# Loading the last 64 rows of a QKV weight into 128 partitions: one transfer or two

## The chip, the cores and the metric

The kernel runs on one core of one Trainium2 chip. The metric is the device time of one execution in microseconds (us). Five engines work side by side: TensorE (PE, matrix products), VectorE (DVE), ScalarE (ACT), GpSimd (POOL) and SyncE (SP). SP computes nothing here; it issues most of the DMA transfers. A core has 16 DMA engines that carry these transfers.

## The reference

One token stream `x` (1 x 2048 x 576, bf16) is normalised, and the same normalised rows feed a local dilated attention and a SwiGLU feed-forward block. The three are added up.

```python
xn = _layernorm(x)                                  # no gain, no bias
# attention: 32 heads of 18; each position looks at 8 positions, 0, 2, ..., 14 back
qkv = (xn @ wqkv)                                   # wqkv: 576 x 1728
logits = einsum("bhsd,bhswd->bhsw", q, kg) * 18 ** -0.5   # masked before position 0
o = einsum("bhsw,bhswd->bhsd", softmax(logits), vg) @ wo
# feed-forward, F = 4608
ffn = (silu(xn @ w_gate) * (xn @ w_up)) @ w_down
return x + o + ffn
```

The contraction length 576 is four blocks of 128 and a rest of 64. The change is in how the rest of `wqkv`, its rows 512 to 575, gets into the on-chip memory.

## The kernel before, in words

The 2048 positions are held as 128 partitions x 16 rows: partition p has positions 16p to 16p+15, and "row r" is the position r of each partition, 128 positions in all. The kernel first computes Q, K and V for all 16 rows (`p_mm`, L310, until about 59.7 us), then runs four rounds of the feed-forward block (`g_pair`, L611, and `d_half`, L640), with the attention of four rows at a time done on DVE beside it (`chain`, L418 to L465). All instructions are issued in the order written (a manual schedule); DVE's attention steps are put between the others by a small planner (`Filler`) that goes by fixed costs.

What matters here is the first 25 us. The transfers, in the order in which they are issued, will be called:

- x0 (on ACT's queue) and x1, x2, x3 (on SP's): the input's rows 0 to 3, one at a time, `load_x`, L145, 128 partitions of 1152 bytes each.
- w1 (on ACT's queue) and w0, w2, w3 (on SP's): the four 128-row blocks of `wqkv`, `load_w`, L149, 128 partitions of 3456 bytes each.
- w4, the last 64 rows of `wqkv`, L152: two transfers, here w4a and w4b, of 64 partitions of 1728 bytes each. The weight's 1728 columns are cut in two halves of 864. The first half goes to partitions 0 to 63 of the tile `wqkvr`, the second to partitions 64 to 127. So PE can use the upper and the lower half of its rows at the same time, each with other output columns.
- c1, c2, c3: the other 12 input rows, L165, 128 partitions of 4608 bytes each.
- The first feed-forward weights, `load_gu(0)`: gate (L182), up (L183) and the two 64-partition rests g8a and g8b (L184, L185); they are first used at 67.1 us.
- Then two zero fills of the K and V rings (L542), and the transposes of normalised rows by DMA (L300): row 0, which is for later, and rows 5, 6, 7, ..., which PE's Q/K/V products need.

SP's order is x1, w0, w2, x2, w3, w4a, w4b, x3, c1, c2, c3, gate, up, g8a, g8b, the zero fills, the transposes. The program gives the DMA transfers eight semaphores in turn; so a transfer also waits, before it is issued, until the one eight places ahead of it has landed.

PE's order at the start: eleven matmuls on constants (`warm_pe`, L174 and L177), the transposes of row 0 (L271), then row 0's products block by block: `p_whole` for w0, w1 and w2, between them the transposes of row 1, four products of row 1 with w0, then four of row 0 with w3 (at 9.37 us) and, as the first use of w4, four half-height products of row 0 (`p_row0_rest`, from 10.20 us). After that `p_row(1, ...)`, `p_row(2)` and so on, 3.3 us each. In `p_row`, w4 is the second block that is used. The products of row 0 are taken out of PSUM by `p_evac(0, ...)` on ACT and DVE as soon as the four half-height products are done.

```python
    def p_row0_rest(t):
        for i in range(2):
            for half in range(2):
                p_mm(t, i + 2 * half, 4, half, 0, False, True)
```

Of the kernel before, what the change touches and what calls it, by code (L numbers as in the profile page):

```python
# [17 lines left out]
P = 128  # L18
H, DH, W, DIL = 32, 18, 8, 2
D = H * DH  # L20
HALF = D // 2
G = 432
# [48 lines left out]
def kernel(  # L71
# [58 lines left out]
    wqkvr = hTf[:, 12 * D:12 * D + 2 * G]  # L130
# [16 lines left out]
    def load_w(eng, kt):  # L147
        if kt < 4:
            eng.dma_start(wqkv[:, kt, :], A_wqkv[kt * P:(kt + 1) * P, :])  # L149
        else:  # L150
            for i in range(2):
                eng.dma_start(wqkvr[64 * i:64 * i + 64, :], A_wqkv[4 * P:D, 2 * G * i:2 * G * (i + 1)])  # L152

    load_x(nc.scalar, 0)
    load_x(nc.sync, 1)
    load_w(nc.scalar, 1)
    load_w(nc.sync, 0)
    make_identity(nc, ident[:])
    load_w(nc.sync, 2)
    load_x(nc.sync, 2)  # L160
    load_w(nc.sync, 3)
# [562 lines left out]
```

## Time and profile before

| | |
|---|---|
| median of 3 runs | 503.4 us (503.15 to 503.45) |
| the profiled execution | 503.37 us, its span 501.6 us |
| PE busy | 497.6 us, 99% of the span |
| DVE, ACT, POOL busy | 329.3 us (66%), 200.9 us (40%), 2.7 us (1%) |
| DMA, mean over the span | 150 GB/s |
| w4a, w4b: 108 KB each, issue to landing | 5.9 and 6.5 us |

The span runs from the first to the last instruction; the time of an execution has about 1.8 us more. Busy times of PE are modelled from pipelined starts, so 99% says that PE has nearly always a matmul under way, not that each runs at its best rate.

### The profile page before, as it was taken

What the parts mean: (1) busy time and instruction counts of PE and PEld (TensorE: products, weight loads), DVE (VectorE), ACT (ScalarE), POOL (GpSimd) and SP (SyncE); (2) the same over time, 40 slices, a digit from 0 to 9 for tenths busy, and PEclk for the clock granted to TensorE, in tenths of its full rate; (3) what the DMA queues carried; (4) which work ended last, traced back from release to release, by engine and by line L of the source; (5) the groups of instructions that cost most, each with busy time, mean ns of one, the idle gap of its engine ahead of it and who ended that gap; (6) DMA issues with size and microseconds to landing.
All of it is one profiled execution on the core that took longest, in us unless ns stands there. A gap on an engine that the chain in (4) does not pass through costs nothing.

```text
span 501.6 us, 13271 instructions
## 1 busy us (share of the span) xinstructions
PE 497.6 (99%) x5795; PEld 283.1 (56%) x5795; DVE 329.3 (66%) x479; ACT 200.9 (40%) x416; POOL 2.7 (1%) x9
## 2 busy tenths in 40 slices
PE   9999999999999999999999999999999999999997
PEld 4555544444677644444777544445777444446775
DVE  5888597898999698999897139995980222221001
ACT  4756657645300255554300445557000454553000
POOL 1000000000000000000000000000000000000000
PEclk9999999999999999999999999999999999999999
DMA  8799989898731045535640154453700335432200
GB/s 311 175 205 238 306 271 293 259 322 260 194 117 61 25 143 189 190 110 177 158 132 29 31 182 153 132 189 110 183 25 14 101 115 177 158 127 39 76 14 25
DMA packets 77186, 75.42 MB, mean 150 GB/s; under 512 B 22708, under 2 KB 72528, under 8 KB 77128
## 3 DMA queue, kind: packets, MB, share of 16 engines
q1 hardware_dynamic: 76840, 73.98, 49.7%
q8 instruction: 45, 0.74, 0.6%
q10 hardware_dynamic: 288, 0.59, 0.3%
q14 instruction: 13, 0.11, 0.1%
HBM read 58.76 MB, written 5.90 MB: 129 GB/s over the span
## 4 chain that ended last, share of the span: by engine, by line
PE 99%; DVE 0%; issue 0%
PE g_ps L611 56%; PE d_ps L640 32%; PE qkv_ps L310 11%; PE warm_ps L174 1%; PE pt L271 0%; DVE ot L654 0%; PE pt L292 0%; PE warm_ps L271 0%; PE warm_ps L177 0%
## 5 line engine op out<-in xcount | busy, mean ns | idle before, releaser
L611 PE MATMUL g_ps<-xnT,gu 64*128 64x512 bf16 x2592 | 280.4, 376 | 0.0
L611 PEld LDWEIGHTS <-gu 64*128 64x128 bf16 x2592 | 126.1, 94 | 152.9
L622 ACT ACTIVATE sg<-g_ps 128x512 bf16<-128x512 f32 x144 | 87.3, 606 | 156.6 <-PE g_ps L611 156.6
L640 PE MATMUL d_ps<-wd,hT 64*128 64x288 bf16 x2304 | 146.3, 283 | 0.0
L640 PEld LDWEIGHTS <-hT 64*128 64x128 bf16 x2304 | 112.0, 94 | 29.8
L624 DVE TENSOR_TENSOR hT<-sg,uc 128x512 bf16<-128x512 bf16 x144 | 60.2, 419 | 93.9 <-ACT uc L623 93.8
L623 ACT CAST uc<-g_ps 128x512 bf16<-128x512 f32 x144 | 85.2, 592 | 0.0
L423 DVE TENSOR_REDUCE PP<-PP 128x64 f32<-128x1152 bf16 x64 | 84.9, 1347 | 0.4
L310 PE MATMUL qkv_ps<-hT,xnT 64*128 64x432 bf16 (+1 forms) x536 | 50.0, 342 | 0.0
L418 DVE TENSOR_TENSOR PP<-QO,Kr 128x2304 bf16<-128x2304 bf16 (+1 forms) x35 | 43.5, 1251 | 7.3 <-DMA Kr<-hT 6.9
L652 DVE TENSOR_TENSOR ot<-d_ps,xr 128x288 bf16<-128x288 f32 x30 | 12.3, 451 | 51.0 <-PE d_ps L640 51.0
L450 DVE TENSOR_TENSOR PP<-Vr,A 128x2304 bf16<-128x2304 bf16 (+1 forms) x35 | 43.3, 1251 | 0.4
L310 PEld LDWEIGHTS <-xnT 64*128 64x128 bf16 (+1 forms) x536 | 26.1, 94 | 22.3 <-ACT xnT L296 0.2
L455 DVE TENSOR_TENSOR PP<-PP 128x2304 bf16<-128x2304 bf16 x24 | 32.5, 1354 | 0.3
L622 ACT ACT_TABLE_LOAD x5 | 6.4, 1283 | 47.2 <-PE g_ps L611 47.2
L640 PE MATMUL d_ps<-wo,xnT 64*128 64x288 bf16 x288 | 22.9, 283 | 0.0
L372 ACT CAST hT<-qkv_ps 128x288 bf16<-128x288 f32 (+2 forms) x58 | 20.9, 423 | 0.0
L443 ACT ACTIVATE PP<-PP 128x1024 f32<-128x1024 f32 x4 | 4.2, 1056 | 31.3 <-DVE PP L439 31.2
L640 PEld LDWEIGHTS <-xnT 64*128 64x128 bf16 x288 | 14.0, 94 | 3.6
L654 ACT CAST ot<-d_ps 128x288 bf16<-128x288 f32 x1 | 0.4, 399 | 38.8 <-PE d_ps L640 38.8
L372 ACT CAST QO<-qkv_ps 128x432 bf16<-128x432 f32 (+1 forms) x30 | 12.2, 406 | 8.3 <-PE qkv_ps L310 8.2
L221 DVE BATCH_NORM_STATS2 stats<-wd 128x6 f32<-128x288 bf16 x32 | 12.8, 440 | 0.0
(56 smaller groups left out, 92.1 us busy)
## 6 DMA issues: line engine op xcount, KB each, us to landing
gu<-in_B_w_gate_dram SPq DMA_DIRECT2D x36, 512.0 KB, 3.8
gu<-in_B_w_up_dram SPq DMA_DIRECT2D x36, 512.0 KB, 5.2
wd<-in_B_w_down_dram SPq DMA_DIRECT2D x9, 576.0 KB, 6.2
kv_d<-hT SPq DMA_DIRECT2D x5, 576.0 KB, 6.1
gu<-in_B_w_gate_dram SPq DMA_DIRECT2D x36, 64.0 KB, 4.9
gu<-in_B_w_up_dram SPq DMA_DIRECT2D x36, 64.0 KB, 4.5
xr<-in_A_x_dram SPq DMA_DIRECT2D x8, 288.0 KB, 3.9
out_dram<-ot SPq DMA_DIRECT2D x16, 144.0 KB, 1.8
```

The source lines that it names most:

```text
L221: nc.vector.bn_stats(sums[r][:, k, :], xc[:, j, k * HALF:(k + 1) * HALF])
L310: return nc.tensor.matmul(t[g][:, 0:G], xT_of(r)[rows, kt, :], w_at(g, kt, rows), start=start, stop=stop)
L372: (nc.vector.tensor_copy if n in dve else nc.scalar.copy)(*parts[n])
L418: nc.vector.tensor_tensor(prod[:, a:b], QO[:, RT * tt + a:RT * tt + b, :], Kr[:, s:s + b - a, :], op=ALU.mult)
L423: nc.vector.tensor_reduce(L[:, w, rs], prod[:, rs].rearrange("p r (h d) -> p r h d", d=DH), axis=AX.X, op=ALU.add)
L450: nc.vector.tensor_tensor(dst[:, a:b], Vr[:, s:s + b - a, :].rearrange("p r (d h) -> p r d h", h=H), A[:, w, a:b].unsqueeze(2).to_broadcas ...
L455: nc.vector.tensor_tensor(dst, acc, pv, op=ALU.add)
L611: mm = nc.tensor.matmul(ring_ps[j][b][:], gu[rows, slot, k, fc], xnT[rows, kt, tok], start=(swap == 0 and kt == 0), stop=(swap == 1 and kt ...
L622: nc.scalar.activation(sg[:], t[0][:], ACT.Silu)
L623: nc.scalar.copy(uc[:], t[1][:])
L624: nc.vector.tensor_tensor(hT[:, ch * FC + j, :], sg[:], uc[:], op=ALU.mult)
L640: mm = nc.tensor.matmul(t[sub][h][:, 0:HALF], a[rows], w[rows, h * HALF:(h + 1) * HALF], start=(swap == 0 and n == 0), stop=(swap == 1 and ...
```

## The change

The two transfers of w4 become one. The source is viewed as two halves of 64 rows of 864 columns, with the half as the outermost index, and the target is the whole tile of 128 partitions.

```diff
@@ -148,8 +148,7 @@
         if kt < 4:
             eng.dma_start(wqkv[:, kt, :], A_wqkv[kt * P:(kt + 1) * P, :])
         else:
-            for i in range(2):
-                eng.dma_start(wqkvr[64 * i:64 * i + 64, :], A_wqkv[4 * P:D, 2 * G * i:2 * G * (i + 1)])
+            eng.dma_start(wqkvr, A_wqkv[4 * P:D, :].rearrange("r (i c) -> i r c", i=2))
```

In the program that is built, the two transfers of before have a source and a target of 64 x 864 elements each. The one that replaces them has a source of 2 x 64 x 864 and a target of 128 x 1 x 864. No other instruction is added, removed or moved on any engine. With one transfer fewer, those that follow take the next semaphore in turn, and PE waits for one semaphore instead of two before the first use of w4.

## The prediction

> **What bounds the kernel now.** I read first the page's busy times and the chain that ended last, for the engine that sets the time.
>
> ```profile
> PE 497.6 (99%) x5795; PEld 283.1 (56%) x5795; DVE 329.3 (66%) x479; ACT 200.9 (40%) x416; POOL 2.7 (1%) x9
> PE 99%; DVE 0%; issue 0%
> ```
>
> The chain is PE from 0.77 us on, without a step that waits for a DMA. So PE can win almost nothing, and whatever makes it wait has no cover: it goes to the end in full. The question is whether w4 still comes in time. I therefore took the timeline of PE and SP at the start, the line of w4's transfers (L152) with its landing times, and the busy times by stretches.
>
> ```profile
> 8.64 0.89 PE L310 MATMUL qkv_ps<-hT,xnT 128*128 128x432 bf16 x4
> 9.37 1.36 PE L310 MATMUL qkv_ps<-hT,PP 128*128 128x432 bf16 x8
> ...
> 3.07 1.34 SPq L152 DMA_DIRECT2D hT<-in_A_wqkv_dram  x2
> ...
> DMA to landing us min/median/max: 5.9/6.2/6.5
> ...
> 6.80:10.20 3.40, 3.40 (x24) 1.81 (x23) 2.71 (x10) 1.23 (x4) 0.74 (x1) 1.00 1.05 327
> 10.20:13.60 3.40, 3.40 (x47) 1.89 (x48) 2.86 (x9) 2.74 (x8) 0.58 (x1) 1.00 1.02 409
> ```
>
> The eight matmuls at 9.37 are row 0's four with w3 and the four half-height ones with w4, which start at 10.20. The two w4 transfers were issued at 3.07 and 3.95, so they land at 9.59 and 9.89 (the trace's semaphore events say the same): 0.3 us before their use. In the stretches PE is busy throughout, and the DMA engines too (shares 1.05 and 1.02). The transfers are bound by their engines, not by their issue: w4 is issued at 3.1 to 4.4, and its first packet starts at 7.56.
>
> **The change part by part.** The sum is made against the profiled execution: 503.37 us, of which 501.6 span; the median of the runs is 503.4, so its differences carry over as they are.
>
> *Over how many engines w4 is spread.* A landing counts 16 on a semaphore, and the trace shows who counts. Transfers whose outermost index runs over 128, 112 or 64 climb by 16 single events, one for each DMA engine. The zero fill L542 has 14 rows in one partition as its outermost index of more than one: its semaphore gets one event early, when the transfer is issued (12.97 us), and then 14 (18.41 to 19.73). So a transfer is cut along its outermost index, and a count of 14 uses 14 engines. The new w4 has an outermost count of 2 in its source and of 128 in its target. No transfer of this trace has different counts on its two sides. If the target decides, it stays at 16 engines; if the smaller or a common divisor decides, it has 2. I take 2, because one piece needs a first row in the source and in the target, and the source is described as two runs of 64 rows: cut in 16 equal shares, the outermost index could not name a share's start. The Trainium skill has this as a rule (page "DMA: Bandwidth & Descriptors", section "Why a DMA increments its semaphore by 16 and not by 1"): the number of engines is the largest up to 16 that divides the slowest dimension of both sides. By that rule it is 2 here, and the 14 events agree with it; its case of unequal sides no run here shows. The same page's table "Rules for kernel authors" advises one 128-partition transfer rather than two on partition halves, which speaks for the change if the transfer stays spread.
>
> *When w4 lands then.* Its 128 packets of 1728 bytes stay. Before, each of 16 engines had 8. The packet records give 72 ns for the fastest and for the first third of them, median 101, mean 106, up to 184 between 8.05 and 8.9 us, when x3 was read beside them. On 2 engines each has 64, one after another. The other 14 go on to x3 and then to the 4608-byte packets, which run at a steady 182 ns, so I take 5 slow ones at 130 ns and 59 at 73: 0.65 + 4.31 = 5.0 us. The bounds are 64 x 72 = 4.6 and 64 x 106 = 6.8 us. The start is where an engine is done with w3: 7.56 to 8.05 us, I take 7.75. From last packet to last landing it took 0.65 us for w4 (9.24 to 9.89), 0.52 for c3 and 0.84 for w3. So w4 lands at 7.75 + 5.0 + 0.65 = 13.4 us; bounds 7.56 + 4.6 + 0.52 = 12.7 and 8.05 + 6.8 + 0.84 = 15.7.
>
> *What PE does.* It reaches the half-height products at 10.1 to 10.2 and waits until 13.4: 3.2 us (2.5 to 5.5). Nothing independent stands ahead in its order: all matmuls behind are row 1's, which stand in the same queue and use w4 themselves.
>
> *PE's clock.* PE starts at half clock: before 6.54 us the starts of 128x432 matmuls are 311 and 357 ns apart, after it 183. And the end of the trace shows what an idle stretch does:
>
> ```profile
> 498.00:501.40 3.40, 0.45 (x8) 0.11 (x4) 0.46 (x1) 0.40 (x1) 0.00 (x0) 1.00 0.12 43
> 501.46:501.57 0.11, 0.00 (x0) 0.00 (x0) 0.00 (x0) 0.00 (x0) 0.00 (x0) 0.50 0.00 0
> ```
>
> The column after POOL's busy time is the granted clock: 3.0 us after the last matmul (end 498.45) it is 0.50. The stall would idle PE from about 10.27 to 13.4, 3.1 us, just as long. So I expect the clock to drop near the stall's end. Getting it back took 5.75 us of matmuls at the start (0.77 to 6.53); at half speed that would lose 2.9 us. A stall so short that the clock holds loses 0. I take the middle, 1.5 us. The Trainium skill ("TensorE: Matmul & The Clock Gate", Part 1) tells of free-running windows of 3.41 us that are judged busy or idle; by that a dropped clock costs one window at half rate, 1.7 us, and whether it drops depends on where the stall lies in a window. The two edges in this trace, 6.525 and 501.458, are 145 such windows apart, which agrees.
>
> *What else moves.* One issue on SP goes (0.47 us): nothing, since issue isn't what the transfers wait for. The semaphores shift by one place only for the eight transfers behind w4. x3 now waits for x0 (landed 3.93), c1 for x1 (3.75 instead of 6.33), c2, c3, gate and up for w1, w0, w2 and x2 (7.6 at the latest), g8a for w3 (9.14): all earlier, and worth nothing, as they queue on the DMA engines anyway. Only g8b is held, for w4 itself, until 13.4 instead of 9.89. Behind it on SP stand the zero fills (until then at 11.64 and 12.64) and the transpose of row 0 (15.88). The fills are issued by about 16.2 then, and the transpose's input comes from DVE behind row 0's evacuation, so it moves with PE to about 19. No one waits.
>
> On the two loaded engines all later shares come about 3.5 us late: x3 lands at about 13.9 instead of 10.24. Its reader on DVE (11.67) stands behind row 0's evacuation, which itself ends at 14.8, so it is covered. c1 lands at about 15.3, its reader moves from 14.46 to 17.7. Row 5's transpose had 1.55 us to spare (landed 21.69, used 23.24) and moves with PE; the backlog on the two engines eats part of that. If the cover were gone here, it would be some tenths of a us. I cost all this at nothing.
>
> **Sum:** 503.4 + 3.2 + 1.5 = 508.1 us.
>
> **The rivals.**
>
> *The clock holds.* The same stall, but PE goes on at full rate: 503.4 + 3.2 = 506.6 (505.9 with the lower bound 2.5). For it: 3.1 us is hardly over the 3.0 that the end of the trace shows, and the end has only the one case. Against it: a stretch of 3.4 us with 0.45 us of work was enough. Chance 0.28.
>
> *The two engines run at the mean packet time of before,* 106 ns, because the two halves of one weight row are still read side by side and others read beside them. The stall is then 5.5 us, surely long enough for the clock: 503.4 + 5.5 + 1.5 = 510.4. Against it: the other engines' packets are long ones after 9 us, at a steady 182 ns, and the first third of w4's ran at 72. Chance 0.14.
>
> *The transfer stays on 16 engines,* cut along the target's 128 partitions. It decides at the point where w4 lands before 10.1 us. Then eight packets per engine as now, landing at about 9.8; PE waits for one semaphore instead of two and can at best start at 10.10, where the last full-height matmul leaves room, instead of 10.20: 503.3 to 503.4, not slower than before, faster by 0.1 at most. That is also the case in which the change does nothing but save an issue. For it: every 128-partition target of this trace has 16 events. Against it: all of those have 128, 112 or 64 on the other side too. Chance 0.11, of which I give 0.02 to a gain that would show, through earlier x3 and c1.
>
> *My forecast,* two engines, stall and clock loss together, 506.9 to 509.5 with the bounds of each: chance 0.47.
>
> **How the numbers follow.** The likeliest case gives 508.1 us. The range takes in the clock that holds (from 505.8, the stall of 2.45) and the slow packets (to 510.5); it leaves out the spread transfer, 0.11, and some 0.07 beyond the ends. A difference of 0.2%, 1.0 us, is about what a measurement of this kernel can tell from none. Faster by more: 0.02. Within: 0.09. Slower by more: 0.89.
>
> **What would show it.** In the profile after, L152's successor (L151) lands 9 to 12 us after its issue, its semaphore has two late events where there were sixteen, and PE has an idle gap before the first L310 matmul with w4, ended by a DMA, at about 10.2 to 13.4. The 1728-byte packets run on past 12 us. If the clock fell, the starts of the L310 matmuls behind the gap are 366 ns apart for 3 us or so, and the granted clock says 0.50 there. The phases after 59.7 us keep their lengths (69.9 and 39.7 us). I am wrong on the first step if sixteen events land before 10.2 us, on the second if the gap is much under 2.4 or over 5.5 us, on the third if the gap alone makes up the difference, and on the covers if a second gap shows between 10 and 60 us.

## The result, and the profile after

| | before | after |
|---|---|---|
| median | 503.35 us (503.15 to 503.45) | 510.83 us (510.28 to 511.08) |
| profiled execution, its span | 503.37, 501.6 us | 510.61, 508.8 us |
| ratio, 95% interval | | 1.0148 (1.013 to 1.0165) |

The one transfer makes the kernel 7.5 us slower. The direction and the mechanism were forecast; the size was not (508.1 us, range to 510.5).

The page's busy times and the chain of after:

```profile
PE 500.1 (98%) x5795; PEld 322.5 (63%) x5795; DVE 329.4 (65%) x479; ACT 201.1 (40%) x416; POOL 2.7 (1%) x9
PE 96%; DMA 2%; SPq 0%; DVE 0%; issue 0%
```

A transfer stands on the chain now. All of it is one piece, as the chain in order of time shows (start, length, what):

```profile
3.23 11.69 DMA hT<-in_A_wqkv_dram
14.96 4.14 PE qkv_ps L309 x22
...
66.91 69.93 PE g_ps L610 x648
136.84 39.69 PE d_ps L639 x648
```

The transfer is w4: issued at 3.23 us, and PE goes on at 14.96. From 66.91 us on, the phases have the lengths of before, so the loss is complete by then. The view of the new transfer's line has its issue and the list of those who waited for it:

```profile
L151 SPq DMA_DIRECT2D hT<-in_A_wqkv_dram x1: 729/729/729, 3.2 to 3.2; - x1
...
  PE qkv_ps L309: 4.8, 1
```

In PE's timeline (the number in brackets is the idle time just before):

```profile
9.28 0.89 PE L309 MATMUL qkv_ps<-hT,PP 128*128 128x432 bf16 x4
...
14.96 0.90 PE L309 MATMUL qkv_ps<-hT,PP 64*128 64x432 bf16 x4 [4.79 <-DMA hT<-in_A_wqkv_dram]
```

Before, the eight matmuls were one piece; now the four half-height ones start 4.76 us later than before (14.96 against 10.20). The rest is in the busy times by stretches, cut at the clock's edges; behind POOL's busy time stand the granted clock, the DMA engines' share and GB/s:

```profile
9.70:13.11 3.41, 0.47 (x3) 0.14 (x2) 0.57 (x2) 0.00 (x0) 0.00 (x0) 1.00 1.04 302
13.12:16.52 3.40, 1.56 (x10) 0.82 (x11) 0.61 (x2) 1.01 (x3) 0.00 (x0) 0.50 1.05 320
16.53:19.94 3.41, 3.41 (x32) 1.75 (x28) 1.57 (x6) 1.20 (x3) 0.58 (x1) 0.50 0.50 133
19.95:23.30 3.35, 3.35 (x48) 2.10 (x46) 3.03 (x11) 1.92 (x6) 0.00 (x0) 1.00 0.14 44
```

The clock halves at 13.11 us and comes back at 19.94. Between 14.96 and 19.94 the pairs of L309 matmuls start 360 ns apart instead of 183. By 19.9 us PE is 7.13 us behind the kernel before, at its last matmul 7.19. So 4.76 us are the wait, the other 2.43 come while the clock is low, and together that is the span's 7.2. An experiment below tells the two apart.

The trace's semaphore events settle how many DMA engines worked, by the reading that the prediction worked out (one event for each engine, and one early event that stands for the missing ones): one early event at 4.34 us, then two, at 14.78 and 14.92. Before there were two times sixteen.

### The profile page after: what moved, and what is told of

It is laid out like the page before. It is cut to its first block, busy times and chain, and to the rows that moved or that the text cites. A ratio compares the mean times of both kernels' runs of the same rounds, so it can differ in the third digit from the quotient of the medians.

```text
span 508.8 us, 13270 instructions
## 1 busy us (share of the span) xinstructions
PE 500.1 (98%) x5795; PEld 322.5 (63%) x5795; DVE 329.4 (65%) x479; ACT 201.1 (40%) x416; POOL 2.7 (1%) x9
## 4 chain that ended last, share of the span: by engine, by line
PE 96%; DMA 2%; SPq 0%; DVE 0%; issue 0%
PE g_ps L610 55%; PE d_ps L639 31%; PE qkv_ps L309 10%; DMA hT<-in_A_wqkv_dram 2%; SPq L149 0%; SPq L145 0%; PE pt L291 0%; DVE ot L653 0%
## 5 line engine op out<-in xcount | busy, mean ns | idle before, releaser
L610 PEld LDWEIGHTS <-gu 64*128 64x128 bf16 x2592 | 143.4, 94 | 135.7
L639 PEld LDWEIGHTS <-hT 64*128 64x128 bf16 x2304 | 127.6, 94 | 14.3
L309 PE MATMUL qkv_ps<-hT,xnT 64*128 64x432 bf16 (+1 forms) x536 | 52.1, 352 | 0.0
L309 PEld LDWEIGHTS <-xnT 64*128 64x128 bf16 (+1 forms) x536 | 30.3, 96 | 20.2 <-issue 1.8
L639 PEld LDWEIGHTS <-xnT 64*128 64x128 bf16 x288 | 15.9, 94 | 1.7
```

The costliest lines, as they stand in the source:

```text
L309: return nc.tensor.matmul(t[g][:, 0:G], xT_of(r)[rows, kt, :], w_at(g, kt, rows), start=start, stop=stop)
L610: mm = nc.tensor.matmul(ring_ps[j][b][:], gu[rows, slot, k, fc], xnT[rows, kt, tok], start=(swap == 0 and kt == 0), stop=(swap == 1 and kt ...
L639: mm = nc.tensor.matmul(t[sub][h][:, 0:HALF], a[rows], w[rows, h * HALF:(h + 1) * HALF], start=(swap == 0 and n == 0), stop=(swap == 1 and ...
```

## The experiments

**How many engines, and why.** Four kernels keep the two transfers of 64 partitions and change only the outermost count of their source, by taking every k-th row together:

```diff
-                eng.dma_start(wqkvr[64 * i:64 * i + 64, :], A_wqkv[4 * P:D, 2 * G * i:2 * G * (i + 1)])
+                eng.dma_start(wqkvr[64 * i:64 * i + 64, :],
+                              A_wqkv[4 * P:D, 2 * G * i:2 * G * (i + 1)].rearrange("(r a) c -> a r c", a=k))
```

k = 2:

> The kernel before with its two w4 transfers of 64 partitions each, but the source rows taken even rows first, then odd ones, so that each transfer's outermost index counts 2 (2 x 32 x 864 to 64 x 864). Left out: the rows' order, so w4's rows stand in other partitions than the products expect; the work on every engine is the same. Theory (the outermost count sets how many DMA engines carry a transfer): two engines, 64 packets of 1728 bytes each, as in the changed kernel; w4 lands at 14.3 to 15.3 us, PE waits 4.3 to 5.2 us, time 510 to 511.5 us. Rival (the cost is of a single transfer over 128 partitions with two runs of rows): 503.4 us, no gap of PE.

k = 16:

> As the run before, but with every 16th row together, so that the outermost index counts 16 (16 x 4 x 864). Left out: the rows' order, as there. Theory (outermost count): 16 engines with 8 packets each as in the kernel before, w4 lands by 10.1 us, 503.2 to 503.6 us. Rival (a source of three indices, or rows that aren't read one after another, is itself slow): over 506 us.

k = 4:

> As the two runs before, with an outermost count of 4 (4 x 16 x 864). Left out: the rows' order, as there. Theory: four engines, 32 packets each; at 72 to 106 ns a packet this takes 2.3 to 3.4 us, so w4 lands between 10.8 and 12.1 us, PE waits 0.6 to 1.9 us, too short for the clock to drop, and the time is 504.0 to 505.3 us. Rival (any transfer on fewer than 16 engines costs about the same fixed time, as by a slow path for the missing engines): 509 to 511 us.

k = 8:

> The kernel before with its two w4 transfers, the source rows taken every 8th together, so that the outermost index counts 8 (8 x 8 x 864). Left out: the rows' order, so w4's rows stand in other partitions than the products expect. Theory (outermost count sets the engines): eight engines with 16 packets each, 1.2 to 1.8 us, so w4 lands at 9.7 to 10.6 us, PE waits 0 to 0.5 us, 503.2 to 503.8 us. Rival (fewer than 16 engines cost a fixed time): 505 us or more.

| outermost count | late events per transfer | last landing of w4 | median | ratio, 95% interval |
|---|---|---|---|---|
| 16 | 16 | 9.60 us | 503.06 us | 0.9999 (0.9989 to 1.0009) |
| 8 | 8 | 10.75 us | 504.02 us | 1.0016 (1.0007 to 1.0026) |
| 4 | 4 | 12.35 us | 506.64 us | 1.0068 (1.0049 to 1.0087) |
| 2 | 2 | 15.97 us | 511.11 us | 1.016 (1.0145 to 1.0175) |

The timeline of PE with k = 2, and with k = 4:

```profile
12.46 0.34 PE L311 MATMUL qkv_ps<-hT,PP 64*128 64x432 bf16 x1 [2.56 <-DMA hT<-in_A_wqkv_dram]
16.01 0.88 PE L311 MATMUL qkv_ps<-hT,PP 64*128 64x432 bf16 x3 [3.21 <-DMA hT<-in_A_wqkv_dram]
```

```profile
10.52 0.34 PE L311 MATMUL qkv_ps<-hT,PP 64*128 64x432 bf16 x1 [0.38 <-DMA hT<-in_A_wqkv_dram]
12.39 0.52 PE L311 MATMUL qkv_ps<-hT,PP 64*128 64x432 bf16 x3 [1.54 <-DMA hT<-in_A_wqkv_dram]
```

There are two waits, one for each half of w4, and they shrink with the count. So neither the number of transfers nor three indices in the source cost anything (k = 16 is the kernel before within 0.1%); the outermost count of 2 costs all of it. The count of 2 landed 0.7 us later than expected, and its waits, 2.56 and 3.21 us, are together longer than the 4.3 to 5.2 expected; its time is inside the expected range. The count of 8 landed 0.15 us later than expected and cost 0.2 us more. The count of 4 missed its expectation: I had held its wait too short for the clock to drop. Two of its four runs had the full clock and took 505.51 and 505.94 us (the timeline above is of one of them), two had a mean clock of 0.997 and took 507.33 and 507.61, 1.75 us more. The wait was a little longer than expected (w4 landed at 12.35 us, not by 12.1), and the statement on the clock was wrong.

**The wait and the clock, apart.** 26 matmuls that add zeros to row 0's sums keep PE busy while w4 is on its way:

```diff
     p_whole(0, t, 3)
+    for i in range(26):
+        nc.tensor.matmul(t[i % 4][:, 0:G], wz[:, 0:P], wqkv[:, 0, 0:G], start=False, stop=False)
     p_row0_rest(t)
```

> The changed kernel with 26 more matmuls of 128x432 ahead of the first use of w4, whose one operand is all zeros and which add nothing to row 0's sums; at 183 ns each they take 4.76 us and keep PE busy while it would wait. Theory (7.2 us are a wait of 4.8 for w4 and 2.5 that PE loses at half clock afterwards): w4 lands at the same time, the clock stays at 1.00, and the time is 508.0 to 508.6 us. Rival (what follows the wait is lost to late transfers on the two loaded engines, not to the clock): 510.3 to 511.1 us as without the added matmuls.

The median is 508.77 us (ratio 1.0111, 1.0096 to 1.0126), 2.06 less than the changed kernel. Two stretches of its span, the wait and the time behind it:

```profile
9.84:14.70 4.86, 4.86 (x27) 2.46 (x26) 0.26 (x2) 0.00 (x0) 0.00 (x0) 1.00 1.03 288
15.20:19.90 4.70, 4.70 (x60) 2.91 (x61) 3.91 (x13) 3.70 (x10) 0.58 (x1) 1.00 0.68 212
```

The clock stays at 1.00 and PE gets through 60 matmuls in the 4.70 us behind the wait, where the changed kernel had 42 from 14.96 to 19.94. The run is a little over the expected range: w4 landed at 15.16 us here, 0.24 later than in the changed kernel's trace, and PE lost another 0.2 at 28.6 us. Two things came last there together: row 5's transpose, whose last event came at 28.59 us, 1.9 us behind its others, and a copy of ACT out of PSUM, which ended at 28.64 and over which the chain runs; the trace can't say which of them alone would have held PE. So the clock is shown to be worth about 2 us, and what else comes late behind the wait some tenths at most.

**Why w4's packets were so slow.** The packet records of after give 72 ns for the first 16 of w4's 128 packets and 96 to 125 for 97 of the other 112 (median 107), mean of all 101. In the same time the 4608-byte packets on the other 14 engines took about 250 ns instead of 182. So I held those back, by a tiny transfer that reads w4's tile and stands ahead of them on SP:

```diff
+    held = const.tile([1, 16], bf16, name="held")
+    nc.sync.dma_start(held[:], wqkvr[0:1, 0:16])
     for c in range(1, 4):
         nc.sync.dma_start(xc_b[c], x_v[:, 4 * c:4 * c + 4, :])
```

> The changed kernel with one tiny transfer added on SP behind x3, which reads 32 bytes of w4's tile and so is issued only when w4 has landed; c1 to c3 and the first feed-forward weights are thereby held back, and beside w4's packets stands x3 alone. Theory (w4's packets on the two engines took 106 instead of 72 ns because c1 to c3 were read beside them): nearly all of w4's packets take 72 to 76 ns, w4 lands at 12.9 to 13.4 us, PE waits 2.8 to 3.2 us, and with the clock lost for some time behind it the run takes 507.6 to 509.4 us. Rival (two engines that each carry 64 such rows are themselves that slow after the first packets): packets at 100 to 110 ns from the ninth on, landing at 14.8 us, 510.3 to 511.1 us.

The median is 508.16 us (507.46 to 509.84; ratio 1.0104, 1.0085 to 1.0124). Nearly every packet took 72 ns (mean 75.6), and w4 landed at 12.71 us, a little ahead of what I had expected. Three of the four runs had a mean clock of 0.997; the one of 509.84 us had 0.993, as the changed kernel, so it lost the clock for longer. The stretches of the profiled run, cut at its clock's edges:

```profile
9.11:12.52 3.41, 1.01 (x6) 0.42 (x5) 0.94 (x4) 0.26 (x2) 0.00 (x0) 1.00 0.13 50
12.53:15.93 3.40, 3.17 (x18) 1.54 (x19) 1.67 (x4) 1.79 (x4) 0.00 (x0) 0.50 0.32 59
```

A DMA share of 0.13 is two engines of sixteen, at 25 GB/s each. PE goes on at 12.76, 2.56 us later than before, and loses 1.55 to one half-rate stretch: 4.1 us. So two engines are not slow by themselves; the neighbours made the difference of 2.2 us in landing. I then put other neighbours there, by moving `load_gu(0)` ahead of c1 to c3:

> The changed kernel with the first feed-forward weights (gate, up and their rests, 1024-byte packets) issued ahead of c1 to c3 (4608-byte packets), so that beside w4 other bytes of another tensor are read. Theory in its narrow form (it is the input's rows, 18432 bytes apart, that slow w4): w4's packets at 72 to 80 ns, landing at 13.0 to 13.6 us, 507.6 to 509.5 us. In its wide form (any transfers on the other 14 engines do): 100 ns and more, landing after 14.5 us, 510 to 511.5 us.

It took 509.65 us (ratio 1.0131, 1.0116 to 1.0146), w4 landed at 14.67, and from 9.05 us on, while gate and up ran beside it, its packets took about 101 ns and theirs about 67 instead of 46. So it is not the input's rows; the wide form holds by the packets and the landing, a little weaker than I had put it (the packets' mean was 94, since the last ones ran with few neighbours). The time lies between the two expected ranges: three of the four runs had a mean clock of 0.997, so they lost it for less time than the changed kernel; the profiled one, 510.37 us, had 0.993.

Two more kernels repeat such loads into dead tiles in the last 40 us of the kernel before, where nothing waits for them:

```diff
+        if tt == NTT - 1:
+            probe()
```

The function `probe`, not printed here, only issues the loads that the expectations list.

> The kernel before with w4 loaded again and again into a dead tile during the last 40 us, when DMA has little else to do and nothing waits for it: first as two transfers, then as one, then as one with c1 to c3 issued behind it, then as one with gate and up behind it; each waits for the one before. Theory: the two transfers land about 2 to 2.7 us after issue; the one alone has 64 packets at 72 ns on each of two engines and lands after 6.2 to 6.9 us; beside c1 to c3 its packets take about 106 ns and it lands after 8.3 to 9.2 us; beside gate and up 72 to 106 ns, as the run with the weights first. Rival (two engines are that slow by themselves): the one alone shows 100 to 110 ns and lands after 8 us or more. The time stays at 503.0 to 503.7 us.

w4 alone as one transfer: 72 ns for 117 of its 128 packets, landed 7.0 us after its issue (469.45 to 476.47), 0.1 more than expected. With c1 to c3 behind it: 72 ns for most packets until 480.0 us, then a median of 107, landed after 8.7 us. Two transfers: 3.2 and 3.5 us, more than expected; loads of `xr` were still ahead of them. With gate and up, 101 of the packets took 72 to 82 ns and 20, between 490.4 and 491.6 us, 94 or more; but there w4 had to wait on its two engines for the backlog of c1 to c3, and much of gate was through by then, so that part tells little. The median is 503.63 us (ratio 1.0008, 0.9997 to 1.0018), no measurable difference.

> The kernel before with other loads into dead tiles during the last 40 us: c1 to c3 alone; then w4 as one transfer with three copies of the same size as c1 to c3 behind it that go from on-chip memory to on-chip memory; then w4 as two transfers with c1 to c3 behind them. Left open so far is where w4's packets and the others' meet: both get slower (72 to 106 ns, 182 to 250 ns) whenever they run side by side. Theory A (they meet in reading HBM): beside the copies w4's packets stay at 72 to 78 ns. Theory B (they meet in writing to the on-chip memory, two engines writing into partitions that the others write too): beside the copies 95 ns or more. In both, c1 to c3 alone show 182 ns. If w4 on 16 engines is followed by c1 to c3, theory A with all reads in step gives 182 ns for the latter once w4 is through. The time stays at 503.0 to 504.0 us.

Beside copies that read no HBM, w4's packets ran at 72 ns until 474.1 us and then took a median of 108, and the copies' packets 255 instead of 178, as with c1 to c3. Theory A falls: they don't need to meet in reading HBM. c1 to c3 alone ran at 178 ns for the most part, with a few packets far above; the part with w4 as two transfers shows w4's packets from 69 to 359 ns and the others' from 175 to over 900 in no order that I can read, so it decides nothing. The median is 503.60 us (ratio 1.0006, 0.9994 to 1.0017).

Theory B fits the numbers, but nothing here shows that the writes are the place; that stays open. These two traces show one thing more: running side by side is not enough. For the first 1.2 us or so, 478.7 to 480.0 and 472.9 to 474.1, most of w4's packets took 72 ns and most of the neighbours' 178 at the same time, and then both slowed down together. What changes at that point is open too.

## Why the prediction was wrong, point by point

- **Two engines** (my first step, and the condition of the rival that kept 16): right. There were two late events, and the row of four counts shows that the outermost count of the source set the number of engines each time, with a target that counts 64 or 128; a smaller count on the target's side was not tried. The Trainium skill ("DMA: Bandwidth & Descriptors", section "Why a DMA increments its semaphore by 16 and not by 1") has the largest number up to 16 that divides the slowest dimension of both sides, and the unequal case, 2 against 128, agrees with it. The Trainium skill's advice in the table "Rules for kernel authors" of "DMA: Bandwidth & Descriptors", one transfer rather than two on partition halves, does not hold here: 510.83 against 503.35 us, because the one transfer's outermost count is 2.
- **When w4 lands**: this step failed by its size. I took 5 slow packets of 64 and 59 at 73 ns, arguing that the neighbours would run "at a steady 182 ns" and so not disturb. In fact three quarters of the packets took 96 ns or more, and the neighbours slowed down too, to about 250 ns. First packet 7.85 us (7.75 forecast), last packet's end 14.07 (12.75), landing 14.92 (13.4). Of the 2.5 us that the sum lacks, 1.6 are this step and 0.9 the clock below. With the neighbours held nearly all packets took the 72 ns, and w4 landed at 12.71, the lower bound.
- **What PE does**: right as a mechanism, since nothing covered the wait: 4.76 us for 3.2, inside its bounds of 2.5 to 5.5.
- **PE's clock**: it dropped, as forecast, at 13.11 us, 2.9 us after the last matmul's end. The loss was 2.43 us where I took the middle of 0 and 2.9, 1.5. The half-rate time was 6.83 us, twice 3.41, of which 1.85 fell into the wait. In the first of these two stretches PE resumed and was busy for 1.56 of 3.40 us, and the clock came back only after the second, in which PE was busy throughout. The Trainium skill ("TensorE: Matmul & The Clock Gate", Part 1) tells of free-running windows of 3.41 us, and these edges agree with it. The estimate from the Trainium skill, one window or 1.7 us, fits the run with the neighbours held (one stretch at half rate, 1.55 us) and not this one.
- **What else moves**: right for PE. There is one gap, and the phases behind keep their lengths. Row 5's transpose stands at a wait of PE only in the run with the filled wait, where 0.2 us were lost, some tenths as I had named them; ACT came last there too, so that it was the transpose is not shown. What I did not have is the long issue of g8a on SP, told below; it cost PE nothing here.
- **The range**: its upper end, 510.5, joined the slow packets with the middle of the clock's loss. The two go together: a longer wait made the drop surer (none or one half-rate stretch with the count of 4, one or two with the neighbours held, two here) and the loss larger. Both upper bounds, 503.4 + 5.5 + 2.9 = 511.8, would have held the 510.83. The rival of the mean packet time, to which I gave 0.14, was nearest with 510.4. Its packets were right in size (106 ns against a mean of 101), but that its sum came so near is partly luck: its wait was 0.7 us too long and its clock loss 0.9 too short.

## What to carry to other kernels

Before two transfers are joined into one, look at the outermost index of both sides as the instruction will carry them: its count says how many DMA engines share the work, and a count of 2 there turned a transfer that landed 0.3 us before its use into one that came 4.7 us late. Where the bounding engine is TensorE and it waits for some microseconds, add the slow clock behind the wait, and add it to the upper end of the range together with the longest wait. A packet time read while all engines run in step is not the packet time of two engines that run beside fourteen others.

## What the runs showed of the hardware that I had not expected

- A transfer of 1728-byte packets on two engines and transfers on the other fourteen slowed each other by 1.4 to 1.5: from 72 to about 107 ns, from 182 to about 250 ns for 4608 bytes, from 46 to about 67 ns for 1024, beside HBM loads and beside on-chip copies alike, but not in the first 1.2 us in the two traces where the end of the kernel gave w4 and its neighbours room.
- SP's own issue became long. The timeline of SP after:

```profile
7.76 2.17 SPq L182 DMA_DIRECT2D gu<-in_B_w_up_dram  x1
9.97 5.87 SPq L183 DMA_DIRECT2D gu<-in_B_w_gate_dram  x1
15.88 0.59 SPq L184 DMA_DIRECT2D gu<-in_B_w_up_dram  x1
```

  The issue of the rest of gate (g8a, L183 here) took 5.87 us instead of 1.23; the semaphore it waits for was free by 8.8 us. It ended at 15.84, 0.9 us after w4 had landed from the two loaded engines. It took 2.56 us with a count of 4 and 0.53 with the neighbours held, so the backlog on the loaded engines is the likely cause, but no run tests it by itself. Nothing that PE needed soon stood behind it here: gate and up are first used at 59.6 us in the kernel before (not at 67.1, as stated there) and at 66.7 after.
- A wait of about 2 us seems enough to drop the clock in some executions (the count of 4: two of four runs, by their mean clock of 0.997 and 1.75 us more; neither was traced). Why only in some is not shown; it fits that the stretches of 3.41 us between clock edges are not tied to the kernel's start, as the first rise to full clock came between 3.4 and 6.7 us in the traces taken. Stretches with PE busy for 0.47 us (after) and 1.01 us of 3.41 (neighbours held) ended with the drop; one with 1.87 us (the count of 4, a run at full clock) did not.
